# Low row blocks by a negated copy and an adding transfer, four loads on another queue, one more held search group

## The chip, the core and the metric

The kernel runs on one core of a Trainium2 chip. The core has five engines with queues of their own: TensorE (PE, matmuls; its weight loads are shown as PEld), VectorE (DVE), ScalarE (ACT), GpSimd (POOL) and SyncE (SP). SP only issues transfers; ACT and POOL can issue them too, and all of them run on the same 16 DMA engines. Each queue runs its instructions in the order in which the program was written; semaphores order the queues against each other. The metric is the device time of one execution in microseconds (us).

## What is computed

Two stages, in float32. First a retention layer (8 sequences of 576 tokens, 8 heads of 64): scores are q times k, scaled and multiplied by a decay that falls with the distance, and 0 above the diagonal; there is no softmax. Its output, 4608 rows of 512, is the input of the second stage, a mixture of 8 experts:

```
logits = x @ w_gate                       # 4608 x 8
walk all (token, expert) pairs from the highest logit down:
    give the token to the expert if the token is free and the expert has under 576 tokens
for each expert e:   out[its tokens] = relu(x[its tokens] @ w1[e]) @ w2[e]     # 512 -> 1024 -> 512
```

So each expert gets exactly 576 tokens, and which ones depends on all the logits. The assignment decides discretely, so the work is done to float32 accuracy: every operand is kept as a high part (rounded to the format that TensorE multiplies fast) and a low part (the rest), and a product is three matmuls: high by high, high by low and low by high.

## The kernel before

**Attention.** Sixteen units (a pair of sequences by a pair of heads) are worked off by `attention` in halves: `A` makes the scores of a half, `within`, `across` and `ST` apply them to v and carry the state from chunk to chunk, `evict` scales the result. `load(u, "kqvn")` (L537 to 548) asks for four tiles of a unit, two units ahead: q and k transposed, v, and k in rows ("n"); each kind has three buffers, so a load waits until the unit three before has been used. SP issues them in the order written, together with the stores of finished rows. The routing's constants are fetched by `R.fetch` (L100 to 103) and the gate's weights by L596, both written where unit 2's first scores are, behind unit 3's loads, and used from the middle of unit 2 on. Of POOL's queue, attention uses only one memset of the gate's tile.

**Routing.** `Route.search(p)` finds expert p's threshold by seven groups of comparisons (its loop over `KK`): VectorE makes a table of 32 candidates (`reach`), TensorE counts with nine matmuls (L351), and VectorE reads the counts and makes the next table. This runs beside the matmuls of the expert before. `Mixer` is the planner that says where: it adds up an estimated time per piece of TensorE's work (`adv`), and writes the next group into the program when its estimate says that the table is ready. A group can be marked as held by the third value of its `yield` (L348): then it is written one piece later, and its own time is added to the planner's clock where it would have stood.

**Experts.** Expert e's first layer is `l1` or, for experts 6 and 7 (`FAST` = 6), `l1_fast`; the second is `l2`, five row tiles of eight pieces. While `l2` of expert e - 1 runs, one thing after another of expert e is written between its pieces: row gathers on POOL (`gather`), weight operands (`feed`), row transposes (`transposes`), and scatters of finished row tiles on POOL. For experts 5 to 7 the rows come in 18 gathers (numbers 0 to 17), at least 1200 ns apart by the planner's clock, and gather g counts as arrived 6000 ns after its issue (`state['at']`, experts 6 and 7).

**Fast first layer.** `l1_fast` multiplies in 28 steps (`STEPS`) with seven products instead of eight for each block of two by two (Strassen's scheme in the Winograd form). It needs seven row blocks of 576 columns, numbered 0 to 6, each high and low; step (i, k) uses block i - 1. `fast_transposes` makes them: six transposes of gathered rows on VectorE, each as soon as its gathers count as arrived; four differences on VectorE (`less`, L1088); seven high blocks on ScalarE (`high`, L1086) and seven low blocks on VectorE (`low`, L1087: rows minus high). Blocks 0 and 1 are plain rows: their high parts follow the third transpose and their low parts the fourth (row groups 9 to 11), before the last gathers. The rest follows the last transpose, in two pieces. The last five low blocks of the two pieces are 2, then 6, 5, 4, 3. The product of a row tile in `l2` takes one of two banks ("y"); ScalarE evacuates it (L1368). The first step of `l1_fast` takes such a bank as well, the one of row tile 3.

**The adding transfer** is in use already for weights: `conv_lo` (L1005, L1006) makes the low part of a weight tile in two steps: ScalarE copies the raw tile with scale -1, which rounds it to the format of the high part, and POOL issues a transfer that adds the raw tile to that copy in memory, which leaves the rest.

Of the kernel before, what the change touches and what calls it, by code (L numbers as in the profile page):

```python
# [11 lines left out]
F32 = mybir.dt.float32  # L12
# [3 lines left out]
ALU = mybir.AluOpType  # L16
AF = mybir.ActivationFunctionType
# [72 lines left out]
class Route:  # L90
# [9 lines left out]
    def fetch(s, nc, fc_d):  # L100
        s.nc = nc
        s.fc = s.pool.tile([128, fc_d.shape[1]], F32, name="rc_f")
        nc.sync.dma_start(s.fc, fc_d)

    def setup(s):

# [216 lines left out]
    def search(s, p):  # L323
# [5 lines left out]
        for it, K in enumerate(KK):  # L329
            last = it == len(SH) - 1  # L330
            v2 = pool.tile([128, 36, 2], BF16, name="v", bufs=2)
            v = v2[:, :, 0]
            if it:

                V.tensor_scalar(v2, u[:, :, None].to_broadcast([128, 36, 2]), j, float(K), op0=ALU.subtract, op1=ALU.mult)
            else:
                V.tensor_copy(v2, s.dg[:, 0, :, None].to_broadcast([128, 36, 2]))
            s.reach(0, 36, K, v2, ALU.is_le)
            if it == 0:
                for k in range(1, 7):  # L340
                    s.dig(k)
                for a, b in ((1, 4), (4, 7)):
                    V.tensor_scalar(s.D[:, a:b], s.dg[:, a:b], 1.0/KK[a], None, op0=ALU.mult)
            if not last:
                u = pool.tile([128, 36], F32, name="u")
                V.tensor_tensor(u, v, s.D[:, it+1], op=ALU.add)

            yield (2050 + 19*K if it else 1350 if p > 1 else 350), 310, (p, it) in ((3, 0), (4, 0), (5, 0), (5, 1), (5, 2), (6, 1))  # L348
            cp = ps.tile([128, 32], F32, name="r")
            for c in range(0, 36, 4):  # L350
                nc.tensor.matmul(cp, s.G[:, c:c+4].rearrange("p c k -> p (c k)"), s.oh[:, c:c+4, :], start=(c == 0), stop=(c == 32))  # L351
            own = [cp[32*c:32*c+32, 8*c:8*c+8] for c in range(4)]

            cs = pool.tile([32, 8], F32, name="cs")
            V.scalar_tensor_tensor(cs, s.nr[:32], -1.0, own[0], op0=ALU.mult, op1=ALU.subtract)
            for x in own[1:3]:
                V.tensor_tensor(cs, cs, x, op=ALU.subtract)
            for q in range(0, 128, 32):
                V.tensor_tensor(s.f[q:q+32, :8], own[3], cs, op=ALU.is_ge)  # L359
            if last:  # L360
                break

            mq = pool.tile([128, 1], F32, name="mq")
            tc, j = pool.tile([128, 32], F32, name="tc"), pool.tile([128, 1], F32, name="j")
            V.tensor_reduce(mq, s.f[:, :8], axis=AX.X, op=ALU.max)
            V.transpose(tc, mq.to_broadcast([128, 32]))
            V.tensor_reduce(j, tc[:, 1:K], axis=AX.X, op=ALU.add)
# [161 lines left out]
def attention(tc, nc, P, qk, vk, cst_d, er_d, wg_d, rf, xd, Lg):  # L529
# [7 lines left out]
    def load(u, what, cuts=None):  # L537

        bp, hp = divmod(u, HP)
        for i in what:  # L540
            n = 1024 if i == "n" else 1152
            t = P['ld'].tile([128, n], F32, name=i + "in", bufs=3)
            src = qk[bp, hp, "qk".index(i)] if i in "qk" else vk[bp, hp, :, :1152] if i == "v" else vk[bp, hp, :, 1152:]
            LD[u, i] = t
            if cuts:
                pieces[u, i] = [(t[:, a:b], src[:, a:b]) for a, b in zip((0,) + cuts, cuts + (n,))]
            else:
                nc.sync.dma_start(t, src)

    pieces = {}  # L550

# [38 lines left out]
    def A(u, hf):  # L590

        if u == 16: return
        if hf == 0 and 2 <= u + 1 < 16:
            if u == 2:
                R.fetch(nc, rf)
                nc.sync.dma_start(wg[:, :, 0:8], wg_d.rearrange("(hp p) e -> p hp e", p=128))  # L596
        pa = two.tile([128, 2, 4, 128], F32, name="pA", tag="A", bufs=1)
        for j in range(4):
            s = slice(512*hf + 128*j, 512*hf + 128*j + 128)
            for r in range(2):  # L600
                nc.tensor.matmul(pa[:, r, j], LD[u, 'k'][half(r), s], LD[u, 'q'][half(r), s], start=True, stop=True, skip_group_check=True)  # L601
        AM[u, hf] = P['w'].tile([128, 2, 4, 128], F32, name="am", bufs=2)
        nc.vector.tensor_tensor(AM[u, hf], pa, m1[:, None, None, :].to_broadcast([128, 2, 4, 128]), op=ALU.mult)  # L603
# [331 lines left out]
def moe(tc, nc, P, R, xd, w1_d, w1q_d, w2_d, out, mix):  # L935
    V, A, T = nc.vector, nc.scalar, nc.tensor
# [143 lines left out]
    def fast_transposes(e):  # L1080
# [3 lines left out]
        xh, xl = [P['s'].tile([128, 7, 2, 288], F32R, name=n, bufs=1) for n in ("xh", "xl")]  # L1084
        XH[e], XL[e] = xh, xl
        high = lambda i, q: A.activation(xh[:, i], x[:, q], AF.Copy)  # L1086
        low = lambda i, q: V.tensor_tensor(xl[:, i], x[:, q], xh[:, i].bitcast(F32), op=ALU.subtract)  # L1087
        less = lambda to, a, b: V.tensor_tensor(x[:, to], x[:, a], x[:, b], op=ALU.subtract)  # L1088
        for g0, g1 in ((0, 4), (4, 8), (8, 9), (9, 12), (12, 16), (16, 18)):
            while not state['force'] and state['at'].get(g1 - 1, mix.t + 1) > mix.t:  # L1090
# [15 lines left out]
        low(2, 3)  # L1106
        less(3, 3, 0)
        high(5, 3)
        less(1, 1, 3)
        yield  # L1110
        high(4, 0)
        high(3, 1)
        for i, q in ((6, 2), (5, 3), (4, 0), (3, 1)):
            low(i, q)
        yield

# [387 lines left out]
```

## Time and profile before

| | |
|---|---|
| time, median of 3 runs | 607.8 us (607.64 to 608.68) |
| the profiled execution | 607.69 us, span 605.9 us, mean granted TensorE clock 0.997 |
| busy: PE, PEld | 590.9 us (98%), 502.9 us (83%) |
| busy: DVE, ACT, POOL | 476.6 us (79%), 298.4 us (49%), 178.6 us (29%) |
| chain that ended last | PE 72%, DVE 12%, issue 7%, DMA 3%, ACT 2%, POOL 2% |
| HBM | 80.21 MB read, 18.87 MB written |

The span runs from the first to the last instruction. Busy shares are means over stages: attention until about 128 us, then the first search, experts 0 to 7 from about 160 us. Expert 6's first layer stands at 499 to 522 us, its second layer until 548, expert 7's first layer until about 571. A line like `L1347 PE MATMUL py<-w2h,hb` names the line of the kernel, the engine, the operation and out<-in by the program's tile names. In a timeline the columns are: start, duration, engine, line, operation, count of merged instructions, and in square brackets the idle time of the engine before it with what ended it.

### The profile page before, as it was taken

To read this page: it belongs to the slowest core of one execution; us is meant where nothing else is said; L and a number is where in the kernel's file an instruction comes from. 1 tells how busy PE (TensorE), PEld (TensorE's weight loads), DVE (VectorE), ACT (ScalarE), POOL (GpSimd) and SP (SyncE) were. 2 spreads that over 40 slices of the span, in tenths; PEclk is the share of its full clock that TensorE was granted. 3 is DMA by queue.
4 is the path that set the end of the run, shared out by engine and by line. 5 is a ranking of instruction groups with operands and counts; after the bars stand their busy time and mean duration, and the time that the engine had idled before them with its cause. 6 is when DMAs were issued, how large, how long until landed. Compare 5 with 4: busy or idle time off the path is not lost.

```text
span 605.9 us, 14929 instructions
## 1 busy us (share of the span) xinstructions
PE 590.9 (98%) x5667; PEld 502.9 (83%) x5667; DVE 476.6 (79%) x1679; ACT 298.4 (49%) x649; POOL 178.6 (29%) x247
## 2 busy tenths in 40 slices
PE   8999999998999999999999999999999999999994
PEld 5888888775698889878977998799889889988973
DVE  3688989898799878977896897799894777888800
ACT  4555555552364446433562447154527448458610
POOL 0000000000511452251332233257737825751021
PEclk9999999999999999999999999999999999999998
DMA  9999999924477699694988298749877724833410
GB/s 323 401 382 337 393 365 401 321 93 152 131 194 149 211 252 231 199 244 148 211 237 238 62 242 217 212 79 240 211 193 161 209 91 125 247 116 96 105 43 35
DMA packets 49775, 125.74 MB, mean 208 GB/s; under 512 B 6160, under 2 KB 20112, under 8 KB 49704
## 3 DMA queue, kind: packets, MB, share of 16 engines
q1 hardware_dynamic: 35812, 79.77, 37.6%
q0 software_dynamic: 13568, 44.58, 32.2%
q8 instruction: 44, 0.72, 0.5%
q10 hardware_dynamic: 324, 0.45, 0.2%
q14 instruction: 27, 0.22, 0.1%
HBM read 80.21 MB, written 18.87 MB: 164 GB/s over the span
## 4 chain that ended last, share of the span: by engine, by line
PE 72%; DVE 12%; issue 7%; DMA 3%; ACT 2%; POOL 2%; POOLq 0%; SPq 0%; ACTq 0%; DVEq 0%
PE py L1347 26%; PE ph L1199 18%; PE pA L601 6%; PE pX L645 5%; PE pS L624 3%; PE ph L1277 3%; PE pX L636 2%; DVE hb L1171 2%; PE pT L683 2%; PE r L351 1%; DVE G L175 1%; DVE f L359 1%; POOL xg L1064 1%; DMA out_y<-yt,idx 1%; PE pT L697 1%
## 5 line engine op out<-in xcount | busy, mean ns | idle before, releaser
L1347 PE MATMUL py<-w2h,hb 128*128 128x512 f32 x576 | 186.7, 396 | 0.0
L1347 PE MATMUL py<-w2l,hb 128*128 128x512 f32 (+1 forms) x320 | 125.1, 391 | 0.0
L1347 PEld LDWEIGHTS py<-w2h,hb 128*128 128x128 f32 x576 | 104.8, 188 | 22.0
L1199 PE MATMUL ph<-xh,w1h 128*128 128x256 f32 (+1 forms) x384 | 111.2, 302 | 0.4 <-ACT xh L1155 0.4
L1199 PE MATMUL ph<-xh,w1l 128*128 128x256 f32 (+1 forms) x384 | 108.9, 296 | 0.0
L1199 PE MATMUL ph<-xl,w1h 128*128 128x256 f32 (+1 forms) x384 | 108.6, 296 | 0.0
L1064 POOL DMA_INDIRECT xg<-xd,idx x25 | 25.5, 1019 | 186.5 <-DMA raw<-in_w 151.9
L1209 ACT ACTIVATE hb<-ph 128x256 fp32r<-128x256 f32 (+1 forms) x96 | 39.1, 408 | 77.4 <-PE ph L1199 75.3
L1199 PEld LDWEIGHTS ph<-xh,w1h 128*128 128x128 f32 x384 | 71.0, 189 | 1.6 <-ACT xh L1155 1.1
L1199 PEld LDWEIGHTS ph<-xl,w1h 128*128 128x128 f32 x384 | 71.3, 190 | 0.2
L1199 PEld LDWEIGHTS ph<-xh,w1l 128*128 128x128 f32 x384 | 71.2, 189 | 0.2 <-DMA w1l<-raw 0.2
L1321 POOL DMA_INDIRECT out_y<-yt,idx x40 | 41.0, 1025 | 95.7 <-ACT yt L1368 77.5
L1347 PEld LDWEIGHTS py<-w2l,hb 128*128 128x128 f32 (+1 forms) x320 | 56.7, 177 | 12.8
L1075 POOL DMA_INDIRECT xg<-xd,quart x54 | 55.3, 1024 | 15.5 <-issue 12.8
L1368 ACT ACTIVATE yt<-py 128x512 f32<-128x512 f32 x32 | 19.0, 592 | 67.2 <-PE py L1347 52.6
L1171 DVE SCALAR_TENSOR_TENSOR hb<-ph,hb 128x256 fp32r<-128x256 f32 (+1 forms) x144 | 42.6, 351 | 9.7 <-ACT hb L1209 9.1
L585 ACT ACTIVATE vin<-vin,cst 128x128 f32<-128x128 f32 (+1 forms) x160 | 48.2, 379 | 3.9 <-DMA cst<-in_cst 2.0
L603 DVE TENSOR_TENSOR am<-pA,cst 128x1024 f32<-128x1024 f32 x32 | 38.9, 1216 | 11.7 <-PE pA L601 11.4
L1277 PE MATMUL ph<-xh,op 128*128 128x288 f32 x224 | 46.4, 299 | 0.6 <-ACT yt L1368 0.4
L1006 POOL DMA_DIRECT2D w2l<-raw x28 | 26.2, 951 | 66.4 <-ACT hb L1209 53.8
L626 ACT ACTIVATE S<-pS 128x128 f32<-128x128 f32 x64 | 17.8, 277 | 44.0 <-PE pS L624 43.9
L601 PEld LDWEIGHTS pA<-qin,kin 64*128 64x128 f32 x512 | 31.1, 187 | 9.3 <-issue 2.8
(215 smaller groups left out, 1121.3 us busy)
## 6 DMA issues: line engine op xcount, KB each, us to landing
raw<-in_w SPq DMA_DIRECT2D x52, 512.0 KB, 5.6
w2l<-raw POOLq DMA_DIRECT2D x28, 512.0 KB, 5.5
w1l<-raw POOLq DMA_DIRECT2D x21, 512.0 KB, 5.9
kin<-in_qk SPq DMA_DIRECT2D x14, 576.0 KB, 7.4
qin<-in_qk SPq DMA_DIRECT2D x14, 576.0 KB, 6.5
vin<-in_vk SPq DMA_DIRECT2D x14, 576.0 KB, 7.6
nin<-in_vk SPq DMA_DIRECT2D x14, 512.0 KB, 8.6
xd<-xr SPq DMA_DIRECT2D x36, 192.0 KB, 6.7
```

Source lines behind the costliest of these rows:

```text
L585: nc.scalar.activation(x, x, AF.Copy, scale=vs[:, u % HP, 4*c+h:4*c+h+1])
L601: nc.tensor.matmul(pa[:, r, j], LD[u, 'k'][half(r), s], LD[u, 'q'][half(r), s], start=True, stop=True, skip_group_check=True)
L603: nc.vector.tensor_tensor(AM[u, hf], pa, m1[:, None, None, :].to_broadcast([128, 2, 4, 128]), op=ALU.mult)
L645: nc.tensor.matmul(PX[u, hf][half(h), b, 128*c:128*c+128], v[:, a:a+64], AM[u, hf][:, h ^ b, j], start=False, stop=False, skip_group_check ...
L1064: nc.gpsimd.indirect_dma_start(out=xg[:n, 4*j:4*j+4, :].rearrange("p a c -> p (a c)"), out_offset=None, in_=xd[:, :], in_offset=bass.Indir ...
L1075: nc.gpsimd.indirect_dma_start(out=XG[e][:, g, :], out_offset=None, in_=xq, in_offset=bass.IndirectOffsetOnAxis(ap=lines[e][:, g:g+1], axi ...
L1171: V.scalar_tensor_tensor(hb[:, f, to+a:to+b], ps[:, a:b], 0.0, hb[:, f, 256*s+a:256*s+b].bitcast(F32), op0=ALU.max, op1=ALU.subtract)
L1199: T.matmul(ps, w, x, start=(k == 0), stop=(k == 11))
L1209: A.activation(hb[:, f, c], ps, AF.Relu)
L1277: T.matmul(ps, a, x, start=(j == 0 and (late or i in (1, 2, 7))), stop=(j == 5), skip_group_check=True)
L1321: st = nc.gpsimd.indirect_dma_start(out=out[:, :], out_offset=bass.IndirectOffsetOnAxis(ap=found[e][:n, t:t+1], axis=0), in_=y[:n], in_off ...
L1347: T.matmul(ps[:m], a, w, start=(k == 0), stop=(k == last), skip_group_check=True)
```

## The change

Four edits: `fetch` and the gate's load move from SP to POOL; so do the n loads of units 6 and 10; group (4, 1) of the search joins the six that are held; and in `fast_transposes` the low blocks 0, 1, 3 and 4 are made by a negated copy on ScalarE and an adding transfer issued by POOL, while 2, 5 and 6 stay on VectorE, 6 and 5 earlier than before.

```diff
@@ -100,7 +100,7 @@
     def fetch(s, nc, fc_d):
         s.nc = nc
         s.fc = s.pool.tile([128, fc_d.shape[1]], F32, name="rc_f")
-        nc.sync.dma_start(s.fc, fc_d)
+        nc.gpsimd.dma_start(s.fc, fc_d)
 
     def setup(s):
 
@@ -345,7 +345,7 @@
                 u = pool.tile([128, 36], F32, name="u")
                 V.tensor_tensor(u, v, s.D[:, it+1], op=ALU.add)
 
-            yield (2050 + 19*K if it else 1350 if p > 1 else 350), 310, (p, it) in ((3, 0), (4, 0), (5, 0), (5, 1), (5, 2), (6, 1))
+            yield (2050 + 19*K if it else 1350 if p > 1 else 350), 310, (p, it) in ((3, 0), (4, 0), (4, 1), (5, 0), (5, 1), (5, 2), (6, 1))
             cp = ps.tile([128, 32], F32, name="r")
             for c in range(0, 36, 4):
                 nc.tensor.matmul(cp, s.G[:, c:c+4].rearrange("p c k -> p (c k)"), s.oh[:, c:c+4, :], start=(c == 0), stop=(c == 32))
@@ -545,7 +545,7 @@
             if cuts:
                 pieces[u, i] = [(t[:, a:b], src[:, a:b]) for a, b in zip((0,) + cuts, cuts + (n,))]
             else:
-                nc.sync.dma_start(t, src)
+                (nc.gpsimd if i == "n" and u in (6, 10) else nc.sync).dma_start(t, src)
 
     pieces = {}
 
@@ -593,7 +593,7 @@
         if hf == 0 and 2 <= u + 1 < 16:
             if u == 2:
                 R.fetch(nc, rf)
-                nc.sync.dma_start(wg[:, :, 0:8], wg_d.rearrange("(hp p) e -> p hp e", p=128))
+                nc.gpsimd.dma_start(wg[:, :, 0:8], wg_d.rearrange("(hp p) e -> p hp e", p=128))
         pa = two.tile([128, 2, 4, 128], F32, name="pA", tag="A", bufs=1)
         for j in range(4):
             s = slice(512*hf + 128*j, 512*hf + 128*j + 128)
@@ -1084,7 +1084,13 @@
         xh, xl = [P['s'].tile([128, 7, 2, 288], F32R, name=n, bufs=1) for n in ("xh", "xl")]
         XH[e], XL[e] = xh, xl
         high = lambda i, q: A.activation(xh[:, i], x[:, q], AF.Copy)
-        low = lambda i, q: V.tensor_tensor(xl[:, i], x[:, q], xh[:, i].bitcast(F32), op=ALU.subtract)
+
+        def low(i, q):
+            if i in (2, 5, 6):
+                V.tensor_tensor(xl[:, i], x[:, q], xh[:, i].bitcast(F32), op=ALU.subtract)
+            else:
+                A.activation(xl[:, i], x[:, q], AF.Copy, scale=-1.0)
+                nc.gpsimd.dma_start(xl[:, i], x[:, q], accum_op=ALU.add)
         less = lambda to, a, b: V.tensor_tensor(x[:, to], x[:, a], x[:, b], op=ALU.subtract)
         for g0, g1 in ((0, 4), (4, 8), (8, 9), (9, 12), (12, 16), (16, 18)):
             while not state['force'] and state['at'].get(g1 - 1, mix.t + 1) > mix.t:
@@ -1106,11 +1112,12 @@
         low(2, 3)
         less(3, 3, 0)
         high(5, 3)
+        low(6, 2)
         less(1, 1, 3)
+        low(5, 3)
         yield
-        high(4, 0)
-        high(3, 1)
-        for i, q in ((6, 2), (5, 3), (4, 0), (3, 1)):
+        for i, q in ((4, 0), (3, 1)):
+            high(i, q)
             low(i, q)
         yield
```

## Rows read from the trace of the kernel before

**Rows 1.** The page's first part: busy us (share of the span) and instructions.
```profile
PE 590.9 (98%) x5667; PEld 502.9 (83%) x5667; DVE 476.6 (79%) x1679; ACT 298.4 (49%) x649; POOL 178.6 (29%) x247
```

**Rows 2.** Windows: stretch, length, busy per engine, clock, DMA share, GB/s.
```profile
core 0: us, PE busy (x) PEld busy (x) DVE busy (x) ACT busy (x) POOL busy (x), PEclk, DMA share, GB/s
4.00:6.00 2.00, 1.91 (x19) 1.08 (x18) 0.05 (x1) 0.14 (x1) 0.00 (x0) 1.00 1.05 370
40.00:72.00 32.00, 31.97 (x644) 25.93 (x640) 28.65 (x64) 17.39 (x60) 0.00 (x0) 1.00 1.02 357
536.00:540.00 4.00, 4.00 (x19) 3.30 (x19) 3.90 (x11) 0.86 (x3) 3.17 (x5) 1.00 0.29 61
```

**Rows 3.** Timeline of the ramp, 0 to 24 us.
```profile
1.05 0.19 POOL L803 MEMSET wg<- 128x128 f32 x1
...
5.86 1.28 ACT L585 ACTIVATE vin<-vin,cst 128x128 f32<-128x128 f32 x4 [1.99 <-DMA cst<-in_cst]
...
9.65 1.75 ACT L585 ACTIVATE vin<-vin,cst 128x128 f32<-128x128 f32 x6 [0.96 <-DMA vin<-in_vk]
...
19.83 0.42 SPq L103 DMA_DIRECT2D rc_f<-in_rf  x1
```

**Rows 4.** Timeline of PE and DVE around search groups (4, 1) and (4, 2).
```profile
309.34 0.39 PE L1347 MATMUL py<-w2l,hb 128*128 128x512 f32 x1
310.02 0.39 PE L351 MATMUL r<-oh,G 128*128 128x32 bf16 x9 [0.29 <-DVE G L175]
...
315.61 0.39 PE L1347 MATMUL py<-w2l,hb 128*128 128x512 f32 x1
315.84 0.39 PE L351 MATMUL r<-oh,G 128*128 128x32 bf16 x9
...
309.20 0.76 DVE L175 TENSOR_TENSOR G<-ct,v 128x1152 bf16<-128x1152 bf16 x1
...
314.00 0.76 DVE L175 TENSOR_TENSOR G<-ct,v 128x1152 bf16<-128x1152 bf16 x1
```

**Rows 5.** Timeline of DVE before expert 7's first layer.
```profile
535.57 1.38 DVE L1087 TENSOR_TENSOR xl<-xt,xh 128x576 fp32r<-128x576 f32 x2
...
542.37 0.45 DVE L1093 STREAM_TRANSPOSE xt<-xg 128x256 f32<-128x256 f32 x1 [0.43 <-DMA xg<-xd,quart]
```

**Rows 6.** Timeline of ACT and PE around expert 6's first layer.
```profile
495.66 0.60 ACT L1368 ACTIVATE yt<-py 128x512 f32<-128x512 f32 x1 [0.20 <-ACT xh L1086]
...
499.12 0.30 PE L1277 MATMUL ph<-xh,op 128*128 128x288 f32 x1
...
522.18 0.63 PE L1347 MATMUL py<-w2h,hb 128*128 128x512 f32 x2
```

**Rows 7.** Timeline of PE and ACT at the start of expert 7's first layer.
```profile
547.46 0.40 PE L1347 MATMUL py<-w2l,hb 128*64 128x512 f32 x1
548.26 0.40 PE L1277 MATMUL ph<-xh,op 128*128 128x288 f32 x1 [0.41 <-ACT yt L1368]
...
545.89 1.83 ACT L1086 ACTIVATE xh<-xt 128x576 fp32r<-128x576 f32 x3 [0.77 <-DVE xt L1088]
547.63 0.58 ACT L1368 ACTIVATE yt<-py 128x512 f32<-128x512 f32 x1
```

**Rows 8.** Timeline of POOL: gathers 16 and 17 of expert 7.
```profile
536.55 1.21 POOL L1075 DMA_INDIRECT xg<-xd,quart  x1 [0.30 <-issue]
538.07 1.04 POOL L1075 DMA_INDIRECT xg<-xd,quart  x1 [0.30 <-issue]
```

**Rows 9.** Line 1006, adding transfers for weights: issue in ns (min/median/max), landing in us.
```profile
L1006 POOL DMA_DIRECT2D w2l<-raw x28: 839/958/1394, 178.2 to 564.0; - x28
...
DMA to landing us min/median/max: 4.6/5.9/9.8
```

**Rows 10.** Windows after the last matmul, columns as in rows 2.
```profile
597.00:598.00 1.00, 0.10 (x1) 0.00 (x0) 0.00 (x0) 0.60 (x1) 0.00 (x0) 1.00 0.00 0
...
600.00:601.00 1.00, 0.00 (x0) 0.00 (x0) 0.00 (x0) 0.00 (x0) 0.00 (x0) 1.00 0.25 94
```

**Rows 11.** Timeline of PE inside expert 7's first layer: its first stall.
```profile
556.23 0.77 PE L1277 MATMUL ph<-xh,op 128*128 128x288 f32 x2
```

## The prediction

> **What bounds the kernel now.** I read the page's first part, then the windows by stage, then the waits, then each engine's timeline at the places that the change touches. TensorE is busy 590.9 us, 98% of the span [rows 1]. So time taken off another engine is worth nothing unless TensorE stands still for it at that place, and an edit that makes TensorE wait costs its full length. In attention TensorE is busy 31.97 of 32 us while the DMA engines are full as well (share 1.02) [rows 2]: no load there can bring more than hundredths. That leaves three places: the ramp at the start, one group of expert 4's search, and the seam between expert 6's second layer and expert 7's first.
>
> The profiled execution took 607.69 us, 1.8 more than its span and 0.1 under the median of the three runs shown. The sum is made on 607.69.
>
> **The four loads.** The router's constants (304.5 KB) and, right behind, the gate (16 KB) go out on SP at 19.83, behind unit 3's loads; only SP's order holds them back [rows 3]. On POOL nothing stands ahead of them but the gate tile's memset at 1.05, and the constants' new tile waits for nobody. So they start near 1.3 us, among the first loads. There the DMA engines are saturated (share 1.05, 370 GB/s [rows 2]), and ScalarE waits for loads: 1.99 until 5.86 for its constants, 0.96 until 9.65 for v [rows 3]. 320 KB at 370 GB/s are 0.89 us of all engines: the upper end. The ramp's warm-up matmuls on TensorE are filler that could take it all: the lower end is 0. The trace has no such overlap; I take +0.4, about the middle, since some of these waits lie on TensorE's path and some beside it. Later TensorE has no idle time to win it back from. What leaves SP's queue at 19.83 moves later loads forward, in a stage where TensorE waits for none: 0. The two n loads (units 6 and 10) keep their wait for the buffer and have POOL to themselves; POOL takes about 0.5 longer for an issue than SP (0.95 for a transfer [rows 9] against 0.42 [rows 3]), under a queue of loads for units not yet begun: 0, at most +0.5.
>
> **The held group.** (4, 1) is expert 4's second search group. The last second-layer matmul before it starts at 309.34, the group at 310.02: 0.68, where the next group starts 0.23 after its forerunner (315.61 to 315.84). It waited for VectorE's table, begun at 309.20 and 0.76 long [rows 4]. Held, it comes one piece later (three matmuls, 0.68), when the table is ready: -0.45. The planner's clock and the next group's due place don't move, since a held group's time is added at the hold. What comes late: VectorE's work on the group's result falls behind one more low block of the expert's rows (about 0.63), so the next table, begun at 314.00 and ready at 314.76, comes near 315.39, and its group stands at 315.84 - 0.45 = 315.39: no new stall beyond hundredths. Bounds -0.45 and +0.2 (0.63 against the 0.45).
>
> **The low blocks.** For experts 6 and 7 VectorE loses four subtractions of 0.69 each (1.38 for two [rows 5]); ScalarE gains four copies and POOL four transfers. The blocks are used by the steps of the first layer, 0.82 us each (28 from 499.12 to 522.18 [rows 6]): 1, 0 and 6 first, 4 in the eighth step, 3 in the thirteenth.
>
> At expert 6's seam TensorE starts at 499.12 with no idle time [rows 6], so VectorE's relief brings 0. The last evacuation that it needs ends at 495.66 + 0.60 = 496.26: a cover of 2.86 against at most the 3.15 found below. 0, at most +0.3.
>
> Expert 7's seam has no cover. TensorE's last matmul starts at 547.46 and the first step at 548.26, released by ScalarE's evacuation of row tile 3 (547.63 + 0.58 = 548.21), whose bank that step takes [rows 7]. In ScalarE's order that evacuation stands behind the high blocks (1.83 for three, 0.61 each), they wait for VectorE's differences, these for the last transpose at 542.37, and that one had waited 0.43 for the last gather [rows 5]. A delay anywhere in this chain delays the first step one for one; the subtractions are not in it.
> - Two of the copies (blocks 4 and 3) stand between the high blocks and the evacuation: 2 x 0.61 = +1.2. Block 6's subtraction, moved ahead of the last difference, holds that up by 0.69, but ScalarE reaches its high block 0.61 later by the first copy and had room: 0, at most 0.1.
> - The transfers of blocks 0 and 1 go where their subtractions stood, after the transpose of row groups 9 to 11. The planner lets that go 6.0 us (of its clock) after gather 11, and gathers go out at least 1.2 apart, so at most gathers 12 to 16 are ahead of it: the transfers stand before gather 17, the last. POOL issues gathers 16 and 17 at 536.55 and 538.07 with only 0.30 between issues, so there is no room [rows 8]. A transfer of this kind holds POOL 0.84 to 1.39, 0.96 at the median [rows 9]; its copy is done in time, ScalarE being busy 0.86 of 4 us there [rows 2]. Two and the usual spacing: +1.95 (1.7 to 2.8). Gather 17 goes at 540.0 and the transpose at 544.3. The transfers' data, ahead of the gather's, may add up to 1.
>
> So the seam costs +3.15, and TensorE starts expert 7 at 551.4 where nothing before it moved, after nearly 4 us of standing still. Next late is block 4's transfer: its copy ends near 549.7 (one copy, one high block, the other copy and the evacuation before 551.4), it lands 4.6 to 9.8 after its issue, 5.9 at the median of 512 KB [rows 9], and it has 288 KB: by 555.6. The eighth step begins at 551.4 + 5.7 = 557.1. The cover is 1.5; at the longest landing 2.4 would be missing. In the standstill the clock should hold: TensorE ends its last matmul of the kernel at 597.1 and is still granted 1.00, the level of 2.4 GHz, from 600 to 601 [rows 10].
>
> **A page against the trace.** POOL's gathers at 536.55 and 538.07 took 1.21 and 1.04 [rows 8] while VectorE was busy 3.90 of 4 us [rows 2]: not held up. The Trainium skill (SBUF — State Buffer, section "SBUF: two separate sides") says that VectorE can lock GpSimd out of a port pair that they share, so that a transfer from the GpSimd queue waits for its descriptors. Its section "A bandwidth-pool intuition that's wrong" puts such a transfer at some 3100 ns instead of 620; an estimate from that page is 6.2 us for two instead of 1.95, and the sum would be near 615. It is a rival below.
>
> **Sum.** 607.69 + 0.4 - 0.45 + 1.2 + 1.95 = 610.8.
>
> **Rivals.**
> - Relief (faster). VectorE decides the seam after all: freed of 1.38 us beside the transposes (the pair at 535.57 [rows 5]), it brings the last transpose forward. That decides if gather 17 has landed before VectorE comes to it. Then 0.57 goes at the seam (0.80 between 547.46 and 548.26 against 0.23), 0.45 at the hold, and the first stall within each of the two first layers (a pair of 0.77 instead of 0.43 [rows 11]), 0.7 in all: 606.0. For it: VectorE is busy nearly throughout before the seam. Against: the 0.43 that it waited for the gather.
> - Copies only. The transfers come to stand behind the last gather: 607.69 + 0.4 - 0.45 + 1.2 = 608.8. Against: the planner's two constants.
> - Nothing to see. The seam takes the copies too (ScalarE has idle time, 3.1 of the 4 us before 540 [rows 2]) and the early loads cost what the hold brings: 607.7. Against: that idle time lies ahead of the chain, not in it.
> - Held-off issue. POOL's issues are stretched beside VectorE as the longest of the row, 1.39, twice: +0.85 on the sum, 611.7, and open above.
>
> **How the numbers follow.** Forecast 0.53, relief 0.18, copies only 0.11, nothing to see 0.11, held-off issue 0.07. What a measurement of this kernel can tell from no change is 0.2%, 1.2 us. Slower by more: the forecast, the held-off issue and a third of copies only, 0.64. Within: nothing to see, the rest of copies only, and 0.04 of relief that stops at the seam and the hold (606.7): 0.22. Faster: 0.14. The forecast's own range is 610.1 (loads 0, issues of 0.84) to 612.3 (loads 0.89, data 1). The whole range goes down to 606.6 for the cases in between, and leaves out the rest of relief and the top of a late landing.
>
> **What would show it.** Right: the router's constants issued by POOL before 2 us, and the score matmuls after the first a few tenths later; group (4, 1) 0.23 after its forerunner; two transfers on POOL between the last two gathers; the last transpose 2 us later against TensorE's second layer; TensorE idle almost 4 us before expert 7's first step, released by the evacuation. Wrong: a first step of expert 7 within 1 us of the matmul before it, or a seam that VectorE releases.

## The result and the profile after

Over five runs each the changed kernel takes 613.38 us at the median (611.53 to 613.47), the kernel before 607.8 (607.07 to 608.68). The ratio is 1.0084, 95% interval 1.0066 to 1.0101: slower, by 5.6 where 3.1 were predicted; the measured time lies 1.1 above the range. The profiled execution took 613.07, 1.99 more than its span, against 607.69, 1.77 more than its own: +5.38.

The seam of expert 7, on four engines in turn. The columns are start, length, instruction, idle time before it and what ended it. The first fence is POOL (the gathers and the adding transfers), the second VectorE, the third ScalarE, the fourth TensorE.

```profile
536.97 0.94 POOL L1075 DMA_INDIRECT xg<-xd,quart  x1 [0.30 <-issue]
537.92 1.95 POOL L1093 DMA_DIRECT2D xl<-xt  x2
540.17 1.06 POOL L1075 DMA_INDIRECT xg<-xd,quart  x1 [0.30 <-issue]
```
```profile
540.65 1.05 DVE L1016 TENSOR_TENSOR op<-raw,op 128x256 fp32r<-128x256 f32 x3
545.38 0.45 DVE L1099 STREAM_TRANSPOSE xt<-xg 128x256 f32<-128x256 f32 x1 [3.68 <-DMA xg<-xd,quart]
```
```profile
550.07 0.67 ACT L1092 ACTIVATE xl<-xt 128x576 fp32r<-128x576 f32 x1
550.65 0.67 ACT L1086 ACTIVATE xh<-xt 128x576 fp32r<-128x576 f32 x1
551.22 0.67 ACT L1092 ACTIVATE xl<-xt 128x576 fp32r<-128x576 f32 x1
551.79 0.57 ACT L1375 ACTIVATE yt<-py 128x512 f32<-128x512 f32 x1
```
```profile
547.69 0.40 PE L1354 MATMUL py<-w2l,hb 128*64 128x512 f32 x1
552.42 0.61 PE L1284 MATMUL ph<-xh,op 128*128 128x288 f32 x1 [4.33 <-ACT yt L1375]
552.82 0.44 PE L1284 MATMUL ph<-xl,op 128*128 128x288 f32 x1
```

Read downwards, in the order of the fences: the two transfers stand between gathers 16 and 17, the last transpose comes 3.01 later than at [rows 5] and waited 3.68 for the gather, the copies at 550.07 and 551.22 hold the evacuation, and TensorE starts 4.16 later than at [rows 7]. And its first matmuls are longer: 0.44 for the one at 552.82. The windows say why (after the stretch: busy time of TensorE, its weight loads, VectorE, ScalarE and POOL, then the granted clock, the share of the DMA engines and GB/s):

```profile
548.00:550.00 2.00, 0.09 (x1) 0.00 (x0) 1.97 (x4) 1.22 (x3) 0.00 (x0) 1.00 0.00 0
550.00:552.00 2.00, 0.00 (x0) 0.00 (x0) 0.88 (x2) 2.00 (x5) 0.95 (x1) 0.69 0.00 0
552.00:554.00 2.00, 1.58 (x6) 1.58 (x7) 0.68 (x1) 0.96 (x2) 0.91 (x2) 0.50 0.82 143
554.00:556.00 2.00, 2.00 (x10) 2.00 (x10) 0.23 (x1) 1.01 (x3) 1.74 (x3) 0.50 0.92 166
556.00:558.00 2.00, 2.00 (x11) 2.00 (x11) 1.46 (x5) 1.28 (x4) 0.34 (x1) 0.60 0.85 219
558.00:560.00 2.00, 2.00 (x17) 2.00 (x16) 0.43 (x2) 1.78 (x4) 0.00 (x0) 1.00 0.64 225
```

TensorE's last matmul ahead of the gap started at 547.69. From 550 to 552 the granted clock is 0.69, then 0.50, the level of 1.2 GHz, and it is still there when TensorE works again: 10 matmuls in a window where 17 fit at 1.00. From its first to its last step the first layer takes 25.36 instead of 23.03.

TensorE in the ramp and in attention, and at the held group:

```profile
21.08 1.16 PE L601 MATMUL pA<-qin,kin 64*128 64x128 f32 x16 [0.55 <-DVE xT L670]
75.73 0.45 PE L624 MATMUL pS<-vin,nin 128*64 128x64 f32 x8 [0.33 <-DMA nin<-in_vk]
310.99 0.39 PE L1354 MATMUL py<-w2l,hb 128*128 128x512 f32 x1
311.22 0.39 PE L351 MATMUL r<-oh,G 128*128 128x32 bf16 x9
```

TensorE's start of each instruction, minus that of the same instruction before, gives the whole account. By 40 us the offset is +0.41 (it was 0.8 after the wait at 21.08, some of which came back), after the wait for unit 6's n +0.96, at the routing +0.95. Up to 305 it falls to +0.59, 0.30 of that at 221, where the kernel before waits for ScalarE's `xh` and this one does not. The held group follows its forerunner by 0.23, as its successor does in [rows 4], and the offset is +0.08: -0.51. A further -0.21 is gone by 480; at expert 6's first step it is +0.04 (+0.17), at the end of its second layer +0.23 (+0.19), at expert 7's first step +4.16 (+3.93), and from the end of that layer to the last matmul +6.49 (+2.33). The end gives back 1.32: from the end of POOL's last issue to the end of the span 5.57 instead of 6.89. 6.49 - 1.32 = 5.17, the difference of the spans; the other 0.2 lies outside them. These are two single executions: a second profile of the kernel before (e13 below) reaches the routing 1.35 later than the first, and by 40 us it is 0.57 later. So the offsets up to the routing are no larger than what the same kernel shows by itself; those at the two seams and at the end come back in other traces.

### The profile page after: what moved, and what is told of

It reads as the page before. It is cut to its first block, busy times and chain, and to the rows that moved or that the text cites. A ratio compares the mean times of both kernels' runs of the same rounds, so it can differ in the third digit from the quotient of the medians.

```text
span 611.1 us, 14954 instructions
## 1 busy us (share of the span) xinstructions
PE 592.6 (97%) x5663; PEld 504.8 (83%) x5667; DVE 471.4 (77%) x1671; ACT 303.0 (50%) x657; POOL 188.8 (31%) x259
## 4 chain that ended last, share of the span: by engine, by line
PE 74%; issue 7%; DMA 6%; DVE 6%; POOL 3%; ACT 3%; POOLq 0%; SPq 0%; ACTq 0%; DVEq 0%
PE py L1354 26%; PE ph L1206 23%; PE pA L601 5%; PE pX L645 4%; DMA nin<-in_vk 3%; PE ph L1284 3%; PE pS L624 3%; PE pX L636 2%; PE r L351 2%; PE pT L683 1%; POOL xg L1075 1%; PE pt L1160 1%; PE pT L697 1%; DMA xg<-xd,quart 1%; POOL out_y L1328 1%
## 5 line engine op out<-in xcount | busy, mean ns | idle before, releaser
L1354 PEld LDWEIGHTS py<-w2l,hb 128*128 128x128 f32 (+1 forms) x320 | 56.7, 177 | 13.2 <-DMA w2l<-raw 0.3
L1284 PE MATMUL ph<-xh,op 128*128 128x288 f32 x224 | 48.4, 308 | 4.5 <-ACT yt L1375 4.3
L1284 PEld LDWEIGHTS ph<-xh,op 128*128 128x128 f32 x224 | 38.3, 197 | 6.1 <-ACT yt L1375 4.8
```

What stands on the lines that cost most here:

```text
L1284: T.matmul(ps, a, x, start=(j == 0 and (late or i in (1, 2, 7))), stop=(j == 5), skip_group_check=True)
L1354: T.matmul(ps[:m], a, w, start=(k == 0), stop=(k == last), skip_group_check=True)
```

## The experiments

Each row is one kernel. Columns: median; median of the kernel before in the same set (runs taken together); ratio with its 95% interval; then from the profile "to 6", the time from the start of the first of expert 5's last 40 second-layer matmuls to expert 6's first step (9.15 without a wait); "gap 7", from the start of the last matmul ahead of expert 7's first step to that step; and "layer 7", from the first to the last start of its first layer.

| kernel | us | before | ratio | to 6 | gap 7 | layer 7 |
|---|---|---|---|---|---|---|
| before | 607.8 | | | 9.15 | 0.80 | 23.03 |
| changed | 613.38 | 607.8 | 1.0084 (1.0066-1.0101) | 9.32 | 4.73 | 25.36 |
| e1 loads, hold | 610.36 | 608.56 | 1.0035 (1.0024-1.0047) | 9.15 | 0.50 | 23.03 |
| e2 low blocks | 616.87 | 608.56 | 1.0126 (1.0104-1.0148) | 13.23 | 4.66 | 25.79 |
| e3 filler at 7 | 617.38 | 608.56 | 1.0128 (1.0100-1.0156) | 13.57 | 4.67 | 23.04 |
| e4 blocks 4, 3 | 609.19 | 608.56 | 1.0004 (0.9987-1.0021) | 9.13 | 1.76 | 23.05 |
| e5 changed | 618.64 | 608.74 | 1.0157 (1.0138-1.0176) | 13.55 | 4.01 | 24.54 |
| e6 blocks 0, 1 | 616.76 | 608.74 | 1.0123 (1.0105-1.0141) | 13.25 | 3.91 | 24.53 |
| e7 late transfers | 619.86 | 608.74 | 1.0184 (1.0169-1.0199) | 15.61 | 4.53 | 24.54 |
| e8 hold | 608.67 | 608.74 | 0.9994 (0.9983-1.0005) | 9.15 | 0.40 | 23.03 |
| e9 filler at both | 617.06 | 608.64 | 1.0129 (1.0109-1.0149) | 11.71 | 4.51 | 23.04 |
| e10 changed | 617.04 | 608.64 | 1.0144 (1.0124-1.0164) | 11.82 | 4.66 | 24.53 |
| e11 block 3 | 609.61 | 608.64 | 1.0012 (0.9996-1.0029) | 9.15 | 0.93 | 23.04 |
| e12 block 3, loads | 610.42 | 608.64 | 1.0029 (1.0015-1.0043) | 9.14 | 0.54 | 23.04 |
| e13 before | 609.42 | 609.16 | one run | 9.15 | 0.58 | 23.04 |
| e14 small transfers | 613.37 | 609.16 | 1.0066 (1.0045-1.0088) | 10.67 | 2.44 | 24.55 |
| e15 hold, 4, 3 | 610.15 | 609.16 | 1.0019 (1.0004-1.0033) | 9.14 | 1.85 | 23.04 |
| e16 eight small | 608.15 | 608.11 | 0.9991 (0.9978-1.0005) | 9.53 | 0.58 | 23.03 |
| e17 six small | 608.64 | 608.11 | 1.0005 (0.9996-1.0014) | 9.50 | 0.69 | 23.05 |
| e18 eight, hold | 608.12 | 608.11 | 1.0001 (0.9989-1.0014) | 9.38 | 0.57 | 23.04 |

**Which part costs: e1, e2, e4, e6.** e1 is the changed kernel with all low blocks on VectorE in the old order, so the four loads and the held group alone; e2 is the kernel before with the low-block edit alone. e4 and e6 change one line of `low` in the changed kernel.

> The changed kernel with all seven low blocks back on VectorE in the old order: the four loads and the held group alone. Seam theory (nearly all of the loss is expert 7's seam: 3.9 us more of standstill and 2.3 for the halved clock after it): the matches of the two traces give +0.95 by the end of attention (0.4 in the ramp, 0.55 where unit 6's n is waited for) and -0.5 at the hold, so 607.8 + 0.95 - 0.5 = 608.2, and TensorE's idle time before expert 7's first step back under 0.6. Rival, spread theory (a good part of the loss is in the loads, and the end only gives some back): 610 or more.

> The kernel before with the low-block edit alone. Seam theory: the whole seam stays, +3.9 standstill, +2.3 clock, -1.2 for the shorter stretch behind the last matmul if that was not chance: 612.8 to 614.0; standstill before expert 7's first step 4.3 and the clock at 0.50 behind it. Spread theory: no more than 611.

The line in e4 and in e6 (the comments name the run):

```
-            if i in (2, 5, 6):
+            if i in (0, 1, 2, 5, 6):      # e4
+            if i in (2, 3, 4, 5, 6):      # e6
```

> The changed kernel with low blocks 0 and 1 on VectorE in their old place, so no transfer stands before gather 17; blocks 4 and 3 stay copies and transfers. Seam theory: the last transpose is back by 3.0, the copies' 1.15 stays, the standstill is 1.5, and the clock holds over it, so 613.4 - 3.0 - 2.3 = 608.1. If the clock falls in a standstill of 1.5 too: 610.4. Rival (the two copies ahead of the evacuation are the main cost and the gather's delay is hidden): 612 or more.

> The changed kernel with low blocks 4 and 3 back on VectorE; 0 and 1 stay copies and transfers ahead of gather 17. Gather theory (the delay of the last gather is the main cost, the two copies ahead of the evacuation only 1.15 of it): TensorE still stands some 3.2 before expert 7's first step and its clock still falls, so 1.2 less than the changed kernel in the same set, 4 or more over the kernel before. Rival, sum theory (the clock goes only with the whole 4.3, so either half alone is cheap): the clock holds, 3.5 less than the changed kernel.

e2 missed upwards: the low-block edit alone costs 8, not 5 to 6, since expert 6's seam costs 4.1 here: TensorE stands 2.5 ahead of expert 5's row tile 4, and the clock falls to 0.50 behind that too. e4 came out as the seam theory has it: blocks 4 and 3 put 1.76 - 0.80 = 0.96 into the gap (1.18 against the 0.58 of e13), the clock stays at 1.00, and the time is that of the kernel before. e6 shows blocks 0 and 1 to carry the loss (+1.23%): both seams wait, and the clock falls although the gap is 0.8 shorter than in the changed kernel's first trace (0.1 shorter than in e5, of its own set). The spread theory is out as the account of the loss, yet e1 is 0.35% over the kernel before, 2.1 where 0.4 was expected: a part that stays open (see e8 to e15).

**The changed kernel again: e5, e10.** No edit.

> The changed kernel once more, on the chip of this set. Its first trace had TensorE through expert 6's seam without a wait, the kernel with the low-block edit alone (616.9) and the one with the filler (617.4) had it wait 2.5 there for ScalarE's evacuation, with the clock at 0.50 behind it: some 4 us. Two-seam theory (both seams hang on the last gather, expert 6's by a cover that a late landing uses up): where the wait is there, the time is 8 over the kernel before; where it is not, 5.5 over. Rival, one-seam theory (expert 6's wait came from what those two kernels changed): 5.5 over, no wait at expert 6's seam.

> The changed kernel beside the one with filler in both standstills, on the same chip. Gather theory with both seams: 8 to 10 over the kernel before, a wait of 2.5 at expert 6's seam, 3.6 to 4.3 before expert 7's first step, the clock at 0.50 behind each. One-seam theory: 5.5 over.

8 to 10 over the kernel before, as the two-seam theory has it: the first pair, with expert 6's seam nearly free, was a mild case. In e10 POOL stands so at expert 6's seam:

```profile
485.11 1.00 POOL L1328 DMA_INDIRECT out_y<-yt,idx  x1 [2.52 <-ACT yt L1375]
486.41 0.98 POOL L1075 DMA_INDIRECT xg<-xd,quart  x1 [0.30 <-issue]
487.38 1.95 POOL L1093 DMA_DIRECT2D xl<-xt  x2
489.64 1.31 POOL L1075 DMA_INDIRECT xg<-xd,quart  x1 [0.30 <-issue]
```

and ScalarE and TensorE:

```profile
484.23 0.60 ACT L1375 ACTIVATE yt<-py 128x512 f32<-128x512 f32 x1 [2.03 <-remote]
499.17 0.58 ACT L1375 ACTIVATE yt<-py 128x512 f32<-128x512 f32 x1
```
```profile
499.80 0.50 PE L1354 MATMUL py<-w2h,hb 128*128 128x512 f32 x1 [2.42 <-ACT yt L1375]
```

ScalarE's evacuation at 484.23 waited 2.03 for something that no row shows ("remote"); POOL's scatter of that tile stands ahead of gather 16, so gather 16 goes at 486.41, where the first trace of the changed kernel has it at 482.65. Then transfers, gather 17, last transpose and high blocks follow, and TensorE's next row tile (the fifth, number 4) needs a bank whose evacuation stands behind them in ScalarE's queue: not the evacuation with 2.86 of cover that the prediction looked at [rows 6], but the one ahead of it, row tile 2's. Here are that evacuation and the matmul that needs it, in the kernel before and then in the first trace of the changed kernel:

```profile
493.43 0.58 ACT L1368 ACTIVATE yt<-py 128x512 f32<-128x512 f32 x1
495.41 0.39 PE L1347 MATMUL py<-w2h,hb 128*128 128x512 f32 x1
```
```profile
494.74 0.58 ACT L1375 ACTIVATE yt<-py 128x512 f32<-128x512 f32 x1
495.37 0.50 PE L1354 MATMUL py<-w2h,hb 128*128 128x512 f32 x1
```

Before, it ended 1.40 ahead of its use; in the first trace of the changed kernel 0.05 ahead, so the cover was used up there already.

**Does the wait come with the chip: e13.** The kernel before, profiled in these sets.

> The kernel before, profiled on the chip of these sets. On it the changed kernel waits at expert 6's seam, on the first chip it did not. Chip theory (ScalarE's wait of 1.3 to 2.5 near 484, whose end no row shows, comes with the chip and uses up the cover of expert 6's seam): the kernel before shows it too, and TensorE runs through that seam (the last 40 matmuls before expert 6's first step take 9.15). Rival, edit theory (the wait comes with one of the edits): no such wait. For the stall of 1.6 near 425, which all but two kernels with the hold show: the kernel before without it speaks for the hold as its cause.

```profile
483.84 0.60 ACT L1368 ACTIVATE yt<-py 128x512 f32<-128x512 f32 x1 [1.16 <-remote]
```

It has ScalarE's wait too, and TensorE passes the seam in 9.15. So that wait is not the edit's. Row tile 2's evacuation ends 0.38 ahead of its use here: the kernel before just absorbs the wait (e1, e8, e11 and e12 absorb waits of 2.0 to 2.1), the changed one can't. Nor does the wait come with the chip: e16 to e18 ran on the chip with the same number and show none.

**The clock: e3, e9.**

```
+        if e == 7:
+            fill = P['bank']("r", [128, 512], "fill")
+            for _ in range(16):
+                T.matmul(fill, P['full'][:, :128], P['full'], start=True, stop=True)
```

e3 has this ahead of expert 7's first step (a further line keeps `full` in `P`). e9 has ten such matmuls ahead of expert 5's row tile 4 as well, at expert 6's seam.

> The changed kernel with 16 matmuls of 128x512 bf16, whose result nothing reads, on TensorE between expert 6's last matmul and expert 7's first step (some 3.7 us at 0.23 each, inside the 4.33 of the standstill; their bank is free). Clock theory (the first steps are slow because the granted clock fell while TensorE stood): the clock stays 1.00 from 552 to 557, the steps keep 0.72 to 0.82 apart, and the time falls by 2.3 to 611.1. Rival, late-operand theory (the first steps are slow since blocks or evacuations come late, whatever the clock): the steps wait for their operands instead and the time stays within 0.5 of 613.4.

> The changed kernel with filler on TensorE in both standstills: 16 matmuls of 128x512 bf16 before expert 7's first step, 10 before expert 5's row tile 4 (the wait ahead of expert 6's seam); nothing reads their result. Clock theory: the standstills stay (2.5 and 4 in sum of filler and idle time), the granted clock stays 1.00 behind both, so the offset against the kernel before no longer grows after either; against the changed kernel in the same set -1.5 to -2.3 for expert 7 and -1.5 for expert 6 where that seam waited: 3 less, 1.5 if only one of them waited. Rival, late-operand theory: the same time as the changed kernel within 0.7.

TensorE in e9:

```profile
552.41 3.63 PE L1244 MATMUL fill<-full 128*128 128x512 bf16 x16
556.68 0.40 PE L1288 MATMUL ph<-xh,op 128*128 128x288 f32 x1 [0.65 <-ACT yt L1383]
556.92 0.29 PE L1288 MATMUL ph<-xl,op 128*128 128x288 f32 x1
```

and the granted clock in e9 and, below, in e10:

```profile
556.00:558.00 2.00, 1.35 (x11) 1.32 (x11) 0.68 (x1) 1.44 (x4) 1.17 (x3) 1.00 0.66 119
558.00:560.00 2.00, 2.00 (x18) 2.00 (x17) 1.11 (x3) 1.72 (x6) 1.47 (x3) 1.00 1.03 178
```
```profile
556.00:558.00 2.00, 1.20 (x5) 1.20 (x6) 0.60 (x1) 1.34 (x3) 1.28 (x3) 0.69 0.60 108
558.00:560.00 2.00, 2.00 (x10) 2.00 (x10) 0.08 (x1) 0.71 (x2) 1.36 (x3) 0.50 1.03 177
```

The gap is the same and the operands are the same, and the first layer takes 23.04 with filler, 24.53 without. In the changed kernel, e2, e5, e6, e7, e10 and e14 the layer takes 24.53 to 25.79, in all others 23.03 to 23.05. The late-operand theory is out: within one execution, the fall of the clock is what lengthens the layer. The low stretch lasts some 6.8 in the changed kernel's first trace and in e2 (layers of 25.36 and 25.79), some 3.4 in e5, e6, e7, e10 and e14 (24.53 to 24.55). In the timed runs the gain isn't shown. e3 came out at 617.38, not 611.1, with expert 6's seam at 13.57; for e9 and e10 the medians are equal, the profiled execution of e9 is 1.56 shorter, the intervals overlap. Nor did the clock fall behind expert 6's seam in e10 (1.00 from 498 to 506), so of the 3 expected only 1.5 was to be had.

The length of a standstill does not tell whether the clock falls. At expert 6's seam TensorE stood 2.42 in e10 and the clock held; it stood 2.49 in e2 and the clock fell, and so it did at that seam in e3, e5 and e6 (2.29 to 2.66) and in e7 (3.50). That is the larger part of why "to 6" is 13.2 to 13.6 in e2, e3, e5 and e6 and 11.8 in e10. e8, the hold alone, lost the clock behind a standstill of 1.72, where e14 kept it behind 1.73 at the same place (near 425). Between two matmuls of one kernel, the clock held behind every standstill of up to 1.62 in these traces and fell behind every one of 2.49 or more without filler; in between, both came. First e10, then e2, then e8 (TensorE, and the window behind); the last window is of the kernel before, just behind [rows 10]:

```profile
500.00:502.00 2.00, 2.00 (x10) 1.35 (x10) 1.22 (x3) 2.00 (x5) 1.90 (x2) 1.00 0.01 2
```
```profile
500.00:502.00 2.00, 2.00 (x6) 1.37 (x5) 0.77 (x3) 2.00 (x5) 1.90 (x2) 0.50 0.25 96
```
```profile
425.19 0.39 PE L351 MATMUL r<-oh,G 128*128 128x32 bf16 x9 [1.72 <-DVE G L175]
426.00:428.00 2.00, 2.00 (x6) 1.56 (x5) 1.82 (x11) 0.63 (x1) 1.39 (x3) 0.51 0.81 164
```
```profile
602.00:603.00 1.00, 0.00 (x0) 0.00 (x0) 0.00 (x0) 0.00 (x0) 0.00 (x0) 0.50 0.00 0
```

**Issue or data: e7, e14.** e7 keeps the four copies and issues the transfers of blocks 0 and 1 behind gather 17. e14 is e4 with two transfers of 4 KB where those of blocks 0 and 1 stood:

```
+                for j in range(2):
+                    nc.gpsimd.dma_start(scr[:, j], xh[:, j, 0, 0:8].bitcast(F32), accum_op=ALU.add)
```

(The lines that make and clear `scr` are left out here.)

> The changed kernel with the transfers of blocks 0 and 1 issued behind gather 17 in place of ahead of it; all four copies stay. Gather theory: the last transpose is back by 3, the standstill before expert 7's first step is 0.41 + 1.15 = 1.6, the clock holds, expert 6's seam has its cover, and the time is within 0.2% of the kernel before with the loads (+0.95) and the hold (-0.5) in it: 0 to 1.5 over it. Rival, transfer theory (the transfers cost by themselves, wherever they stand, by their data or by landing late for the first steps, which use blocks 1, 0 first): 3 or more over it, with TensorE waiting for xl.

> The changed kernel with blocks 0 and 1 on VectorE and, in place of their transfers, two adding transfers of 4 KB each into a tile that nothing reads, ahead of gather 17 as these were. Issue theory (two thirds of the gather's delay is the time in which POOL issues the two transfers): gather 17 about 2 later than in the same kernel without them, the gap before expert 7's first step 1.8 + 2.0 = 3.8 instead of 4.7, the clock falls still: 2 less than the changed kernel. Rival, data theory (it is the 576 KB that the transfers move, not their issue): the gap is within 0.5 of 1.8 and the time of the kernel with transfers of blocks 4 and 3 alone, 0 to 1 over the kernel before.

VectorE in e7, then POOL and VectorE in e14:

```profile
550.01 0.45 DVE L1101 STREAM_TRANSPOSE xt<-xg 128x256 f32<-128x256 f32 x1 [0.32 <-DMA xg<-xd,quart]
553.57 1.55 DVE L1096 TENSOR_TENSOR xt<-xt 128x576 f32<-128x576 f32 x2 [3.12 <-DMA xl<-xt]
```
```profile
541.49 1.22 POOL L1075 DMA_INDIRECT xg<-xd,quart  x1 [0.30 <-issue]
542.72 1.95 POOL L1110 DMA_DIRECT2D scr<-xh  x2
544.97 1.26 POOL L1075 DMA_INDIRECT xg<-xd,quart  x1 [0.30 <-issue]
```
```profile
547.88 0.45 DVE L1099 STREAM_TRANSPOSE xt<-xg 128x256 f32<-128x256 f32 x1 [0.98 <-DMA xg<-xd,quart]
```

My expectation for e7 fell. The last transpose is on time, and VectorE's next difference waits 3.12 for the transfers: `less(0, 2, 0)` overwrites the block that a transfer still reads. As a reader of `xt` a transfer holds up whoever writes it next, and this stood in no theory of mine. It is the slowest kernel of all. e14 fell between its two theories: POOL is held for the same 1.95, but from gather 16's issue to the last transpose it takes 6.39, against 5.82 in the kernel before, 5.69 in e4 and 8.41 in the changed kernel. Over all traces that time is 5.5 to 5.8 in the eleven with nothing between the two gathers and 8.4 to 8.8 in the seven with both transfers there. So the issue time costs 0.6 to 0.9 and the transfers' 576 KB 2.0 to 2.4 (e14 is one trace). Counted to the transpose that waits for it, gather 17 lands 2.9 after the start of its issue in e14, 4.3 before, 5.2 in the changed kernel: part of the longer issue is made up in flight. A row of POOL gives the issue alone. The Trainium skill (Perfetto Trace Analysis, section "DMA Instruction — SWDGE (GPSIMD)") says that the shown end of such a transfer is that of its descriptors' making, not of its data. The rows agree: e7's two issues end at 551.82, VectorE waits for them until 553.57.

**The hold and the loads: e8, e11, e12, e15.** e8 is `(4, 1)` alone. e11 adds block 3 alone, copied after the evacuations; e12 adds the four loads to that; e15 is e4 without the loads.

> The kernel before with the held group alone. Hold theory: group (4,1) follows its forerunner at 0.23, 0.45 to 0.5 under the kernel before, which lies inside what can be measured (ratio 0.998 to 1.000); in the trace the offset drops by 0.5 at 310 and stays. Rival, pushed-on theory (the stall moves to the next group): no drop.

> The kernel before with the held group, and of the low-block edit only block 3, whose copy stands behind row tile 3's evacuation, with its transfer behind all gathers. So no copy or transfer is ahead of the first step; block 3 is used in the thirteenth. Ending theory (the stretch from POOL's last issue to the end of the span was 6.9 to 7.4 in the three traces without transfers of this kind and 5.3 to 5.6 in the seven with them, so they shorten it): 1.3 to 1.9 there and 0 to 0.45 of the hold, 1.3 to 2.3 under the kernel before (ratio 0.996 to 0.998), the stretch near 5.5. Rival, chance theory (the stretch has nothing to do with them): within 0.5 of the kernel before.

> The same with the four loads on GpSimd's queue. Load theory (as predicted, with the n loads at the upper end that was found: 0.4 in the ramp, 0.55 at the waits for n): 0.5 to 1 more than the kernel without them in the same set. Rival (loads and hold alone were 2.1 over the kernel before, the hold alone 0.1 under, so the loads cost 2): 2 to 2.5 more.

> The kernel before with the held group and with blocks 4 and 3 alone by copy and transfer, no loads. With the loads in it was 609.2 against 608.6. Load theory (the loads cost 1 there): 608.2, so -0.4 to -0.9 against the kernel before, ratio 0.9985: the gap before expert 7's first step stays 1.76 against 0.80, and the stretch behind POOL's last issue is 5.5 against 6.9. Rival (the loads cost nothing by themselves): 609.2 again.

```
+    def last_low(e):
+        x = XT.pop(e)
+        A.activation(XL[e][:, 3], x[:, 1], AF.Copy, scale=-1.0)
+        nc.gpsimd.dma_start(XL[e][:, 3], x[:, 1], accum_op=ALU.add)
```

This is the copy and the transfer of e11 and e12, called ahead of the first step.

e8: the stall ahead of group (4, 1) is gone, the time is the same, and a stall of 1.72 stands ahead of a group of the next expert. In e1, where it is 1.62:

```profile
422.05 0.15 DVE L355 SCALAR_TENSOR_TENSOR cs<-room,r 32x8 f32<-32x8 f32 x1 [2.05 <-remote]
```
```profile
424.82 0.39 PE L351 MATMUL r<-oh,G 128*128 128x32 bf16 x9 [1.62 <-DVE G L175]
```

VectorE and ScalarE both stand 2 there, again for something without a row. It is in 11 of the 15 traces that have the hold, and in none of the five without it (e18's expectation counts eight of ten; it was 11 of 14 by then). But of those five only e2 and e13 are from sets in which any such waits without a row occur. That the hold brings it about is possible and not shown. In e8 this new stall takes more than the hold gave.

What the loads cost stays open. e1 against e8 gives 0.41%, across two sets; e12 against e11 gives 0.17%, about 1, with overlapping intervals; e4 against e15 gives -0.15%, overlapping too, so the gain expected of e15 without the loads (0.9985) did not come: 1.0019.

**The end: e16, e17, e18.**

```
+            if u == 5:
+                scr = P['c'].tile([1, 8, 8], F32, name="scr")
+                for j in range(8):
+                    nc.gpsimd.dma_start(scr[:, j], wg_d[j:j + 1, :])
```

e16 is the kernel before with these eight transfers, e17 with six of them, e18 with the eight and the held group.

> The kernel before with eight more DMAs of 32 bytes each, issued by GpSimd in the middle of attention into a tile that nothing reads. Count theory (the stretch from the end of POOL's last issue to the end of the span follows the number of DMAs that POOL issues: 6.8 to 6.9 with none added, 7.0 with two, 7.2 to 7.4 with four, 7.5 with six, 5.3 to 5.5 with eight, 5.5 to 5.6 with twelve): the stretch is 5.3 to 5.5, the time 1.4 under the kernel before, ratio 0.9977. Rival, kind theory (adding transfers of blocks do it, by what they do in the seams): the stretch stays 6.9 and the time the same.

> The same with six of them. Count theory: the stretch is 7.5, the time 0.6 over the kernel before, 2 over the kernel with eight. Kind theory: 6.9, the same time as with eight.

> Eight of them and the held group: the parts of the change that may bring something, without those that cost. Count theory: 1.4 under the kernel before for the stretch; the hold 0 to 0.45 more, less where the stall of 1.6 near 425 comes with it (it stood in eight of ten traces with the hold and in neither of the two profiles of the kernel before): between 606.5 and 608 where the kernel before takes 608.6.

The count theory is refuted: the stretch behind POOL's last issue is 7.02, 6.98 and 7.02. No kernel beats the one before by more than its interval.

## Why the prediction was wrong

- **The step that failed: "In the standstill the clock should hold".** Priced at 0, measured +2.33 in the first layer (1.5 to 2.8 over the traces in which the clock fell there). The gap itself was foreseen (TensorE "after nearly 4 us of standing still"; 4.33 measured), and rows from the end of the kernel [rows 10] were taken to cover it: there the clock was 1.00 from 600 to 601 behind a last matmul that ended at 597.1, here it was 0.69 from 550 to 552 behind one that started at 547.69. One observation of a held clock was taken for a bound. The trace of the kernel before shows the fall just behind the rows that were read (0.50 from 602 to 603, above), and over the twenty traces it comes 2.4 to 5.3 behind the end of the last matmul. With 2.3 the sum would have been 613.1; that this is so near to 613.38 is partly luck, since the other misses below cancel.
- **Gather 17: right in place, wrong in kind.** +1.95 for issue in the sum, "up to 1" for data in the range alone; the transpose came 3.01 later, 1.06 more than the sum has, and 0.6 to 0.9 of it is issue and 2.0 or more data (e14). One term was too long and the other left out, so the range met it by cancelling errors.
- **Copies: right.** +1.2; from the first high block behind the last transpose to the evacuation 5.93 instead of 4.79, +1.14.
- **Expert 6's seam: wrong cover.** Priced 0, at most 0.3; +0.17 in the first trace, 2.6 to 6.5 in the other traces that issue both transfers of blocks 0 and 1, the clock's fall included where it fell. The cover of 2.86 belonged to row tile 3's evacuation; row tile 2's came first, with 1.40 in the trace that was read and 0.38 in e13. The small +0.17 was luck.
- **Loads: not shown either way.** The first trace has +0.41 by 40 us, as priced, and +0.55 at unit 6's n, just above the upper end given. But the same kernel before differs by 0.57 by 40 us between its two profiles, and of the eleven traces with the loads only that one and e5 wait for unit 6's n; e11, without the loads, waits 0.68 for an n elsewhere.
- **Hold: right in its place** (-0.51 against -0.45), but the next group does not keep its place: it too comes a piece later, at 316.59, which hides that its table is ready at 315.93 and not near 315.39. And "no new stall beyond hundredths" does not stand in most other traces.
- **Not in the sum:** the end's -1.32, -0.57 between the routing and expert 6, and +0.19 within expert 6.
- **The rivals.** Held-off issue: the two transfers took 1.95, within 0.02 in every trace, so nothing was held off; that its 611.7 lies nearer to 613.38 than the forecast does is luck. The Trainium skill (SBUF — State Buffer, section "A bandwidth-pool intuition that's wrong") gives its 3100 ns for a transfer beside a `tensor_copy` of VectorE. The estimate of 6.2 carried that over to the TENSOR_TENSOR work that VectorE does here, and the trace doesn't show it there. Relief did not come: VectorE, freed, waited 3.68 for the gather. "Copies only" describes e4, whose transfers of 0 and 1 are gone, and which took 609.2 where the kernel before took 608.56. "Nothing to see" fell with the copies.

## What to carry to other kernels

Where an edit makes TensorE stand still, price what the clock does behind the gap as a term of its own, with a bound of its own, and not from one stretch elsewhere that happened to hold; gaps of nearly one length held the clock in one execution and lost it in another. Work of one engine that is turned into a DMA on another's queue costs three things: its issue there, its bytes ahead of the next transfer's, and its hold on the buffer that it reads; rows of the queue show the first alone. A cover has to be counted from each instruction that waits in that queue, the earliest needed first, and against delays that one trace doesn't show.

## What the runs showed of the hardware

The stretch from the end of POOL's last issue to the end of the span has two levels, and they sort by the packets that the page of the profile gives for POOL's queue: 6.89 to 7.55 in the ten traces with 13568 to 14256 packets, mostly higher with more, 5.27 to 5.57 in the ten with 14544 to 15120. Nothing here tried it by packets alone (e16 to e18 added only 192 to 256), so the cause stays open. In the sets of e1 to e15 ScalarE, and near 425 VectorE too, waits 0.7 to 2.5 for an event without a row, at the same few places (near 305, 352, 422 and 484), though not at each in every trace; in the first pair and in e16 to e18 there is none. The cause stays open.
